# Attention with padded leftover keys, fixed banks and a written order, ahead of two expert stages

## The chip, the core and the metric

The kernel runs on one core of a Trainium2 chip. The core has TensorE (PE; its weight loads are PEld), VectorE (DVE), ScalarE (ACT), GpSimd (POOL), and SyncE (SP), which issues most DMAs. Each runs its own queue in order. The metric is the device time of one execution in microseconds, lower is better.

## The reference

```python
def _attn_ref(q, k, v):                     # each (4, 8, 576, 64)
    # rotate q and k by position (cos and sin tables over the two halves of 64)
    scores = scale * np.matmul(q_rot, k_rot.transpose(0, 1, 3, 2))
    scores = scores - np.max(scores, axis=-1, keepdims=True)
    attn = np.exp(scores)
    attn = attn / (np.sum(attn, axis=-1, keepdims=True) + 1e-09)
    return np.matmul(attn, v)

def _moe_ref(x, w_gate, w_val, w_out):      # x (2304, 512), weights to 1536
    gate = 1.0 / (1.0 + np.exp(-(x @ w_gate)))
    return gate * (x @ w_val) @ w_out

def _moe2_ref(x, w_gate, w1, w2):           # 8 experts, one for each token
    # choose the expert by argmax of x @ w_gate; out = its weight * relu(x @ w1[e]) @ w2[e]
```

The attention's result, with its heads side by side, is the 2304 x 512 input of the gate stage, whose result is the input of the routed experts.

## The kernel before

Every product is made of rounded operands: a value is split into a high part (`hi`, a cast to the rounded type) and a low part (`lo`, the difference), and two or three products are added in PSUM.

The attention works on 16 pairs of heads (`Pair`). Each kind of work on a pair is a piece with a letter:

- `L` loads q, k or v; `K` and `A` rotate k and q (`rope`), `D` copies the rotated k beside itself, `B` and `C` make q's high and low parts, `w` and `G` those of v (tile `vs`).
- `q0` to `q4` transpose the rotated k and q on TensorE, `c` and `b` split the result into `kh` and `kl` and cast it to `qz`.
- `s0` to `s8` are the scores of 128 queries against 576 keys (`s8`: the last 64 queries of both heads), two products for each half of 288 keys. `m` is the row maximum on VectorE, `e` the exponential on ScalarE, which also gives the row sums.
- `t0` to `t10` transpose the probabilities P, `h` casts them to `Th`, `d` takes the difference `Tl`. `t1` and `t6` are those of the last 64 queries, which lie for head 0 on rows 0 to 63 and for head 1 on rows 64 to 127 of one tile (`p` in the rows).
- `v` (head 0) and `o` (head 1) are the output products, ten for each half of 288 queries. The 576 keys are four blocks of 128 rows (tiles `Tha`, `Thb`) and 64 leftover keys of both heads, one above the other in one tile (`Thc`, `Tlc`). So the first two of the ten are products with 64 rows. A half group of five is `v0`, `v1` and so on.
- `z`, `r`, `y`, `Y`, `Z` bring the reciprocal sums through DRAM (`rd`, `rb`) to the layout of the output, `l`, `a`, `F` finish it (`x`), `X` stores it to `xs` in DRAM. `U` is a step of the preparation of the gate stage's first weights.

The order is written by hand as tables of pieces with a lag in pairs (`FIRST`, `STEADY`, `LAST`) and holds for all five engines. PSUM has eight banks: two that rotate for P (`tp`), twice two for scores (`S`), two for q, k and outputs (`O`). The rotation tables (`tab`, four planes) come in three DMAs, and all first loads go through SP's queue.

The gate stage (`moe1`) takes x from `xs` in tiles of 384 tokens (`xr`, split into `xh` and `xl`) and multiplies with weights that are loaded as 64-bit words (`wraw`) and decoded on VectorE. Its first block is three tiles. SP's order and the other engines' order behind the attention are a scheduler's.

Of the kernel before, what the change touches and what calls it, by code (L numbers as in the profile page):

```python
# [11 lines left out]
F32 = mybir.dt.float32  # L12
# [23 lines left out]
FIRST = """  # L36
    s5:1 F:2 A:-1 e4:1 q3:0 m5:1 h4:2 c3:0 s6:1 t5:3 d10:3 b1:0 h9:3 d6:2 m6:1 e5:1 q2:0 h8:3 l3:3 s7:1 m7:1
    e6:1 q4:0 s8:1 m8:1 h7:3 D:-1 h5:2 t2:1 B:-1 c4:0 c2:0 v0:3 t10:3 h10:2 e7:1 w:0 C:-1 d7:2 h6:3 Lq:-2 b4:0
    h2:1 d2:1 v2:3 t3:1 s0:0 o2:3 m0:0 t0:1 h3:1 d8:2 U:2 e8:1 d4:3 K:-2 o3:2 h0:1 d3:1 Y:2 e0:0 X:3 s1:0 m1:0
    Lk:-3 d5:3 Lv:0 z:1 a3:2 t4:3 a2:3 q0:-1 s2:0 d0:1 e1:0 t1:1 a0:2 v3:2 h1:1 l1:2 t6:3 t7:2 d9:2 q1:-1 a1:2  # L40
    r:1 s3:0 t8:3 c0:-1 y:1 G:0 o1:3 Z:2 m2:0 e2:0 d1:1 v1:2 l0:2 o0:3 s4:0 m3:0 t9:3 e3:0 l2:2 c1:-1 b0:-1 m4:0
"""
STEADY = """
    D:-1 A:-1 t4:2 h4:2 s5:1 b1:0 t5:2 q4:0 e4:1 F:3 q3:0 d4:2 c4:0 h5:2 s6:1 c3:0 t7:2 b4:0 m5:1 h7:2 q2:0 v0:2
    d5:2 B:-1 m6:1 t6:2 e5:1 Y:2 h6:2 d7:2 e6:1 K:-2 v1:2 X:3 s7:1 t10:2 d6:2 t9:2 Lq:-2 l0:2 U:1 c2:0 s8:1
    Lk:-3 m7:1 h10:2 a0:2 d10:2 e7:1 h9:2 q0:-1 v2:2 m8:1 t8:2 c0:-1 s0:0 d9:2 v3:2 e8:1 h8:2 l1:2 s1:0 G:1
    b0:-1 m0:0 Z:2 t0:1 d8:2 e0:0 m1:0 o0:2 Lv:-1 h0:1 e1:0 a1:2 w:0 t1:1 s2:0 o2:2 d0:1 t3:1 s3:0 m2:0 h1:1
    h3:1 o1:2 e2:0 C:-1 z:1 d1:1 t2:1 m3:0 l2:2 d3:1 h2:1 e3:0 o3:2 s4:0 a2:2 d2:1 m4:0 r:1 l3:2 q1:-1 y:1 c1:-1
    a3:2
"""  # L50
# [1257 lines left out]
```

## Time and profile before

| what | us |
|---|---|
| median of three runs | 1125.86 (1122.24 to 1130.41) |
| the profiled execution | 1121.85 |
| its span, first to last instruction | 1120.1 |
| TensorE busy in the span | 1085.5 |
| VectorE busy | 739.7 |
| ScalarE busy | 544.1 |
| GpSimd busy | 308.5 |

The times are device time; the profile is of one execution, and its span is measured from its first instruction. An engine's busy time is the time in which at least one of its instructions was being executed. The matmuls are pipelined, so that printed lengths on TensorE overlap.

### The profile page before, as it was taken

The page shows a single profiled execution, that of the slowest core. Times are in us where ns is not written, and L with a number is a line of the kernel's source. Part 1 is how long each engine was busy: PE and PEld are TensorE (multiplying, and loading weights), DVE is VectorE, ACT ScalarE, POOL GpSimd, SP SyncE. Part 2 cuts the span into 40 slices and gives each one's busy share as a digit, 9 for nine tenths or more (in the row PEclk, how much of TensorE's full clock was granted, in tenths as well). Part 3 has the DMA queues.
Part 4 walks back from the last instruction along what each step waited for, and adds up shares of the span by engine and source line. Part 5 has one row for each costly group of instructions (what it writes and reads, how often), then busy time and mean ns, then how long its engine had stood idle before and what let it go on. Part 6 is the DMA issues. An engine that isn't in the chain of part 4 may idle for free. (4 is left out here: it accounts for less than half of the span.)

```text
span 1120.1 us, 18566 instructions
## 1 busy us (share of the span) xinstructions
PE 1085.5 (97%) x6349; PEld 962.2 (86%) x6349; DVE 739.7 (66%) x1581; ACT 544.1 (49%) x1164; POOL 308.5 (28%) x281
## 2 busy tenths in 40 slices
PE   6999999999999999999999999999999999999993
PEld 6889888888889999997889999987778888888882
DVE  5898888888887887876657655555672333846620
ACT  4888888888884222233221222232233444856631
POOL 6967576675211000000100100001215322222200
PEclk8999999999999999999999999999999999999997
DMA  6434233341125344342134332120122615757400
GB/s 176 107 80 112 65 107 104 85 108 54 54 71 163 114 148 126 121 137 61 30 67 74 105 108 81 57 85 20 49 67 59 226 45 183 262 179 288 148 20 19
DMA packets 86101, 116.74 MB, mean 104 GB/s; under 512 B 29727, under 2 KB 71071, under 8 KB 81904
## 3 DMA queue, kind: packets, MB, share of 16 engines
q1 hardware_dynamic: 80864, 104.08, 30.2%
q0 software_dynamic: 5136, 11.40, 3.1%
q8 instruction: 52, 0.85, 0.4%
q14 instruction: 49, 0.40, 0.2%
HBM read 168.33 MB, written 15.70 MB: 164 GB/s over the span
## 5 line engine op out<-in xcount | busy, mean ns | idle before, releaser
L646 PE MATMUL z<-xh,zh 128*128 128x384 f32 x576 | 194.1, 337 | 0.0
L646 PE MATMUL z<-xl,zh 128*128 128x384 f32 x576 | 193.7, 336 | 0.0
L729 POOL DMA_INDIRECT idx<-tokid,pi x18 | 19.6, 1086 | 433.7 <-DVE pi L728 372.5
L646 PE MATMUL z<-xh,zl 128*128 128x384 f32 x576 | 123.8, 336 | 0.3 <-DVE zl L554 0.3
L202 DVE TENSOR_REDUCE nm<-S 128x1 f32<-128x576 f32 x144 | 107.8, 749 | 21.4 <-PE S L199 20.4
L646 PEld LDWEIGHTS z<-xl,zh 128*128 128x128 f32 x576 | 108.2, 188 | 0.9 <-DVE xl L528 0.8
L646 PEld LDWEIGHTS z<-xh,zh 128*128 128x128 f32 x576 | 108.2, 188 | 0.1
L646 PEld LDWEIGHTS z<-xh,zl 128*128 128x128 f32 x576 | 101.9, 188 | 0.9 <-DVE zl L554 0.9
L211 ACT ACTIVATE P<-S,nm 128x576 f32<-128x576 f32 x128 | 95.4, 745 | 7.5 <-DVE nm L202 6.4
L652 ACT ACTIVATE sg<-z 128x384 f32<-128x384 f32 x72 | 35.2, 489 | 117.3 <-PE z L646 106.7
L653 DVE TENSOR_TENSOR g<-z,sg 128x384 f32<-128x384 f32 x72 | 40.0, 556 | 75.1 <-PE z L646 75.1
L670 PE MATMUL xm<-oh,gh 128*128 128x512 f32 x216 | 88.5, 410 | 0.0
L670 PE MATMUL xm<-oh,gl 128*128 128x512 f32 x216 | 84.6, 392 | 0.0
L670 PE MATMUL xm<-ol,gh 128*128 128x512 f32 x216 | 84.5, 391 | 0.0
L199 PE MATMUL S<-kh,qz 128*128 128x288 f32 x320 | 78.3, 326 | 4.2 <-ACT P L211 3.2
L527 ACT CAST gh<-g 128x512 fp32r<-128x512 f32 x54 | 33.3, 621 | 91.8 <-PE xm L670 87.2
L249 PE MATMUL tp<-ident,P 128*128 128x128 f32 x512 | 74.8, 274 | 0.3 <-DVE Tla L270 0.3
L1124 PE MATMUL y<-w2h,hh 128*128 128x512 f32 x176 | 72.5, 412 | 1.7 <-ACTq L1144 0.9
L1009 DVE TENSOR_TENSOR xl<-tp,xh 128x512 fp32r<-128x512 f32 x21 | 14.5, 691 | 85.2 <-ACT xh L1008 48.9
L1124 PE MATMUL y<-w2l,hh 128*128 128x512 f32 x176 | 69.4, 394 | 0.0
L1124 PE MATMUL y<-w2h,hl 128*128 128x512 f32 x176 | 68.9, 392 | 0.0
L199 PE MATMUL S<-kl,qz 128*128 128x288 f32 x320 | 68.8, 296 | 0.0
(241 smaller groups left out, 2648.4 us busy)
## 6 DMA issues: line engine op xcount, KB each, us to landing
raw<-in_moe_w_dram SPq DMA_DIRECT2D x100, 1024.0 KB
wraw<-in_moe_w_gate_dram SPq DMA_DIRECT2D x23, 512.0 KB
wraw<-in_moe_w_val_dram SPq DMA_DIRECT2D x23, 512.0 KB
wraw<-in_moe_w_out_dram SPq DMA_DIRECT2D x12, 512.0 KB
rb<-rd SPq DMA_DIRECT2D x32, 144.0 KB
xs<-x SPq DMA_DIRECT2D x16, 288.0 KB
xr<-xs SPq DMA_DIRECT2D x24, 192.0 KB
ldk<-in_k_dram SPq DMA_DIRECT2D x16, 256.0 KB
```

The lines of the kernel that those rows point to most:

```text
L199: nc.tensor.matmul(ps[:, c, 0:288], st, t[:, 288 * c:288 * c + 288], start=(n == 0), stop=(n == len(ops) - 1))
L202: nc.vector.tensor_reduce(out=self.nm[:, u:u + 1], in_=self.S[u][:, :, 0:288], axis=AX.XY, op=ALU.max, negate=True)
L211: nc.scalar.activation(out=p.rearrange("p (a b) -> p a b", a=2), in_=self.S[u][:, :, 0:288], func=AF.Exp, bias=self.nm[:, u:u + 1], accum_ ...
L249: nc.tensor.transpose(ps[:, 128 * i:128 * i + 128], P[i][:, h, c:c + 128], ident)
L527: nc.scalar.copy(out=hi, in_=src)
L646: nc.tensor.matmul(p[:, 0:TN], a[:, 128 * c:128 * c + 128], b[:, c], start=(n == 0), stop=(n == 11))
L652: nc.scalar.activation(out=sg, in_=z[0], func=AF.Sigmoid)
L653: nc.vector.tensor_tensor(out=g[i][:, f], in0=z[1], in1=sg, op=ALU.mult)
L670: nc.tensor.matmul(p, a[:, c], b[f], start=(f == 0 and m == 0), stop=(f == NF - 1 and m == 2))
L729: nc.gpsimd.indirect_dma_start(out=idx, out_offset=bass.IndirectOffsetOnAxis(ap=pi, axis=0), in_=tokid[:, blk:blk + 1], in_offset=None)
L1009: self.nc.vector.tensor_tensor(out=lo, in0=src, in1=hi, op=ALU.subtract)
L1124: nc.tensor.matmul(py, a[:, c], b[:, c], start=(c == 0 and m == 0), stop=(c == 7 and m == 2))
```

## The change

- The 64 leftover keys of a head are padded to a block of 128 rows. v is loaded to a tile of two times five blocks with zeros in the other head's half (`ldv`), so that a leftover product takes all 128 rows of `Thc` with `vs` zero in the other head's rows. The leftover queries of both heads are transposed together in full 128-row blocks (`t1`, `t6`), and the transpose of the sums (`r`) becomes the third block of `t6`, its copy (`y`) a part of `h6`. For this `kh` and `kl` keep the shared leftover keys twice (one more copy in `c4`, one more difference in `b4`).
- The rotating PSUM tiles become four single banks and two double ones, and each piece has its bank in the order (`/n`).
- The order is one written list of 1675 pieces for all pairs.
- Only the two planes of k's rotation table are loaded; ScalarE makes q's from them and copies them for the second head. The small first loads of k and q go out on ScalarE's queue. Pair 0's q is rotated in two parts (`J`, `I`, `N` are the second head's).
- v's high part for all pairs but the first is cast on GpSimd (`W`), and so are both parts of the gate stage's first weights.

```diff
-FIRST = """
-    s5:1 F:2 A:-1 e4:1 q3:0 m5:1 h4:2 c3:0 s6:1 t5:3 d10:3 b1:0 h9:3 d6:2 m6:1 e5:1 q2:0 h8:3 l3:3 s7:1 m7:1
...
+ORDER = """
+    K.0 J.0 A.0 D.0 Lk.2 q1.0/0 q0.0/1 c1.0 Lq.2 B.0 b1.0 K.1 c0.0 C.0 W.0 b0.0 q2.0/2 I.0 q4.0/3 G.0 c2.0 c4.0 N.0 Lv.2
...
+    t10.15/2 h7.15 d6.15 v0.15/1 h10.15 d7.15 X.14 t9.15/3 d10.15 t8.15/0 h9.15 v1.15 h8.15 d9.15 v2.15/2 l0.15 d8.15 v3.15
+    Z.15 a0.15 o0.15/3 l1.15 o1.15 a1.15 o2.15/0 l2.15 o3.15 a2.15 l3.15 a3.15 F.15 X.15
...
-    ps_t = ctx.enter_context(tc.tile_pool(name="a_pt", bufs=2, space=PSUM))
-    ps_s = ctx.enter_context(tc.tile_pool(name="a_ps", bufs=2, space=PSUM))
-    ps_o = ctx.enter_context(tc.tile_pool(name="a_po", bufs=2, space=PSUM))
+    ps = ctx.enter_context(tc.tile_pool(name="a_ps", bufs=1, space=PSUM))
+    BANK = [ps.tile([128, 512], F32, name=f"bank{i}") for i in range(4)]
+    BANKS = [ps.tile([128, 2, 512], F32, name=f"banks{i}") for i in range(2)]
...
+        def L_(self, nm, parts=(0, 1), g=nc.sync):
+            src = {"q": q, "k": k, "v": v}[nm]
+            s = src[self.b, 2 * self.hp:2 * self.hp + 2]
+            if nm == "v":
+                t = ldv[self.i % 2]
+                nc.sync.dma_start(out=t[:, :, 0:4].rearrange("p h u d -> p h (u d)"),
                                   in_=s[:, 0:512].rearrange("h (p u) d -> p h (u d)", u=4))
+                for h in range(2):
+                    nc.sync.dma_start(out=t[64 * h:64 * h + 64, h, 4], in_=s[h, 512:576])
+                return
...
+        def W_(self, n):
+            self.vs = sb_o.tile([128, 10, 2, 64], F32R, tag="vs", name="vs", bufs=3)
+            src = ldv[self.i % 2].rearrange("p h u d -> p (h u) d")
+            if self.i == 0:
+                nc.scalar.copy(out=self.vs[:, :, 0], in_=src)
+            else:
+                nc.gpsimd.tensor_copy(out=self.vs[:, :, 0], in_=src)
...
         def t_(self, g):
-            ps = self.tp[g] = ps_t.tile([128, 512], F32, tag="tp", name="tp")
+            ps = self.tp[g] = BANK[self.slot]
+            blocks = lambda n: ps[:, 128 * n:128 * n + 128]
...
-            elif g == 1 or g == 6:
-                h = 0 if g == 1 else 1
-                p = slice(64 * h, 64 * h + 64)
+            elif g == 1:
+
                 for j in range(4):
-                    c = 64 + 64 * h + 128 * j
-                    nc.tensor.transpose(ps[:, 64 * j:64 * j + 64], P8[p, c:c + 128], ident[p, p])
-                c = (576, 0)[h]
-                m = (64, 128)[h]
-                nc.tensor.transpose(ps[0:m, 256:320], P8[p, c:c + m], ident[p, p])
+                    nc.tensor.transpose(blocks(j), P8[:, 128 * j:128 * j + 128], ident)
+            elif g == 6:
+
+                nc.tensor.transpose(blocks(0), P8[:, 512:640], ident)
+                nc.tensor.transpose(blocks(1), P8[:, 448:576], ident)
+                nc.tensor.transpose(ps[0:9, 256:384], self.r, ident)
...
         def v_(self, n, h=0):
...
-                if j == 4:
-                    p = slice(64 * h, 64 * h + 64)
-                    st, mv = self.vs[p, 8], T[2][p, cs]
-                else:
-                    st, mv = self.vs[:, 4 * h + j], T[h][:, j, cs]
+                mv = T[2][:, cs] if j == 4 else T[h][:, j, cs]
+                st = self.vs[:, 5 * h + j]
...
-        nc.sync.dma_start(out=tab[:, 2:4, 4:9], in_=rope_tab[:, 2:4])
-        p0.load("k")
-        nc.sync.dma_start(out=tab[:, 0:2, 4:9], in_=rope_tab[:, 0:2])
-        p0.load("q")
-        p1.load("k")
-        nc.sync.dma_start(out=tab[:, :, 0:4], in_=rope_tab[:, :, 0:4])
+        nc.sync.dma_start(out=tab[:, 2:4, 4:9], in_=rope_tab)
+        p0.L_("k", (1,), nc.scalar)
+        p0.L_("k", (0,))
+        p0.L_("q", (1,), nc.scalar)
+        p0.L_("q", (0,))
+
+        nc.scalar.mul(out=tab[:, 0:2, 4:9], in_=tab[:, 2:4, 4:9], mul=SCALE)
+        nc.scalar.copy(out=tab[:, 2:4, 0:4], in_=tab[:, 2:4, 4:8])
+        nc.scalar.copy(out=tab[:, 0:2, 0:4], in_=tab[:, 0:2, 4:8])
...
+        for piece in ORDER.split():
+            x, i, slot = (piece.replace("/", ".") + ".-1").split(".")[:3]
+            i = int(i)
+            pairs[i].slot = int(slot)
+            getattr(pairs[i], x[0] + "_")(x[1:] if x[0] == "L" else int(x[1:] or 0))
...
-        self.steps += [lambda: nc.scalar.copy(out=w.hi, in_=val),
-                       lambda: nc.vector.tensor_tensor(out=w.lo, in0=val, in1=w.hi, op=ALU.subtract)]
+        self.steps += [lambda: nc.gpsimd.tensor_copy(out=w.hi, in_=val),
+                       lambda: nc.gpsimd.tensor_tensor(out=w.lo, in0=val, in1=w.hi, op=ALU.subtract)]
```

In the steady part TensorE's queue of the kernel before has, in one place, a half of the outputs of head 1, the leftover transposes of one head and the next scores:

```order
L309 MATMUL O<-Thc,vs 128x288
L309 MATMUL O<-Tlc,vs 128x288
L309 MATMUL O<-Thb,vs 128x288
L309 MATMUL O<-Tlb,vs 128x288
L309 MATMUL O<-Thb,vs 128x288
L241 MATMUL tp<-ident,p_112 128x64 x4
L244 MATMUL tp<-ident,p_112 64x64
L199 MATMUL S<-kh,qz_111 128x288 x2
L199 MATMUL S<-kl,qz_111 128x288 x2
```

A like place of the changed kernel on TensorE, where the outputs lie in bank 102 and the leftover transposes in bank 100:

```order
L420 MATMUL bank_102<-Thc,vs 128x288
L420 MATMUL bank_102<-Tlc,vs 128x288
L420 MATMUL bank_102<-Thb,vs 128x288
L420 MATMUL bank_102<-Tlb,vs 128x288
L420 MATMUL bank_102<-Thb,vs 128x288
L274 MATMUL bank_99<-ident,rk 128x128
L274 MATMUL bank_99<-ident,rq 128x128
L363 MATMUL bank_100<-ident,p_112 128x128
L364 MATMUL bank_100<-ident,p_112 128x128
L365 MATMUL bank_100<-ident,r 9x128
```

The five small transposes became two full ones and that of the sums; the number of output products is the same.

At the end of the attention SP's queue of the kernel before reads x for the gate stage (`xr`) between the attention's own transfers:

```order
L292 DMA rb<-rd 64x576 x2
L634 DMA xr<-xs 128x384 x8
L373 DMA xs<-x 128x576
L634 DMA xr<-xs 128x384 x3
L542 DMA wraw<-in_moe_w_gate_dram 128x4x256
L542 DMA wraw<-in_moe_w_val_dram 128x4x256
L285 DMA rd<-rt 4x2x128
L286 DMA rd<-rt 2x1x64
```

and SP's queue of the changed kernel there:

```order
L400 DMA rd<-rt 4x2x128
L401 DMA rd<-rt 2x1x64
L447 DMA xs<-x 128x576
L407 DMA rb<-rd 64x576 x2
L703 DMA xr<-xs 128x384 x4
L611 DMA wraw<-in_moe_w_gate_dram 128x4x256
L611 DMA wraw<-in_moe_w_val_dram 128x4x256
L447 DMA xs<-x 128x576
L611 DMA wraw<-in_moe_w_gate_dram 128x4x256
L703 DMA xr<-xs 128x384
L838 DMA wglr<-in_moe_w_gate_dram 128x4x8
L703 DMA xr<-xs 128x384 x7
```

The last sums' write and read (`rd`, `rb`) moved ahead of all xr loads, and eight of the twelve stand behind the last store of x.

## Rows read from the trace of the kernel before

**Rows 1.** Busy time by stage: us, each engine (instructions), clock, DMA share, GB/s.

```profile
0.00:20.00 20.00, 12.98 (x82) 11.82 (x83) 9.45 (x25) 6.55 (x12) 9.87 (x17) 0.89 0.67 199
...
100.00:200.00 100.00, 99.35 (x729) 88.22 (x727) 86.87 (x160) 86.47 (x217) 68.96 (x61) 1.00 0.35 95
```

**Rows 2.** Waits from 60 to 330 us: us in total, times, longest.

```profile
DVE nm L202 <- PE S L199: 15.2, 26, 0.7
...
PEld tp L249 <- DVE Tla L270: 0.8, 2, 0.6
```

**Rows 3.** Timeline of TensorE in one pair: start, length, what, count.

```profile
192.44 0.29 PE L309 MATMUL O<-Thb,vs 128*128 128x288 f32 x1
192.66 0.46 PE L241 MATMUL tp<-ident,p 64*128 64x64 f32 x4
...
193.47 0.42 PE L199 MATMUL S<-kl,qz 128*128 128x288 f32 x2
193.83 0.40 PE L309 MATMUL O<-Thc,vs 64*128 64x288 f32 x1
...
194.66 0.29 PE L309 MATMUL O<-Thb,vs 128*128 128x288 f32 x1
194.79 0.60 PE L249 MATMUL tp<-ident,P 128*128 128x128 f32 x4
...
195.50 0.43 PE L199 MATMUL S<-kl,qz 128*128 128x288 f32 x2
...
196.42 0.60 PE L249 MATMUL tp<-ident,P 128*128 128x128 f32 x4
...
198.06 0.27 PE L274 MATMUL tp<-ident,r 128*9 128x128 f32 x1
198.16 0.60 PE L146 MATMUL O<-ident,rk 128*128 128x128 f32 x4
```

**Rows 4.** Line 149 (one a pair) from 60 to 310 us: first and last start.

```profile
L149 PE MATMUL O<-ident,rk x13: 272/273/273, 60.7 to 299.6; 128*128 128x128 f32 x13
```

**Rows 5.** Timeline of VectorE in the steady stretch.

```profile
102.33 0.68 DVE L270 TENSOR_TENSOR Tla<-tp,Tha 128x512 fp32r<-128x512 f32 x1
102.93 0.75 DVE L202 TENSOR_REDUCE nm<-S 128x1 f32<-128x576 f32 x1
```

**Rows 6.** Timeline of the head; in brackets idle time before and what ended it.

```profile
1.75 0.72 SPq L105 DMA_DIRECT2D ldk<-in_k_dram  x1
...
4.67 0.69 DVE L122 TENSOR_TENSOR rk<-ldk,tab 128x512 f32<-128x512 f32 x1 [3.09 <-DMA ldk<-in_k_dram]
...
7.34 0.23 DVE L122 TENSOR_TENSOR rk<-ldk,tab 128x64 f32<-128x64 f32 x1 [1.31 <-DMA ldk<-in_k_dram]
...
9.02 0.69 DVE L122 TENSOR_TENSOR qs<-ldq,tab 128x512 f32<-128x512 f32 x1 [0.45 <-DMA ldq<-in_q_dram]
...
15.11 0.71 PE L146 MATMUL O<-ident,rq 128*128 128x128 f32 x4 [2.51 <-DVE kl L181]
...
19.05 0.85 PE L199 MATMUL S<-kh,qz 128*128 128x288 f32 x2 [1.01 <-ACT qz L174]
```

**Rows 7.** Change-over to the gate stage: timelines, and line 646 by stage.

```profile
324.86 11.69 SPq L634 DMA_DIRECT2D xr<-xs  x8
...
330.52 0.51 ACT L527 CAST xh<-xr 128x384 fp32r<-128x384 f32 x1
...
344.58 0.67 SPq L285 DMA_DIRECT2D rd<-rt  x1
...
345.88 0.29 PE L309 MATMUL O<-Tlb,vs 128*128 128x288 f32 x1
...
347.02 1.15 SPq L292 DMA_DIRECT2D rb<-rd  x2
...
356.50 0.55 DVE L653 TENSOR_TENSOR g<-z,sg 128x384 f32<-128x384 f32 x1
...
330.00:346.00 16.00, 4.74 (x19) 3.22 (x20) 1.00 0.57 171
```

More of the change, by code (lines that the diff above doesn't have):

```diff
@@ L61 @@
+"""
+FIRST_HEAD = (slice(0, 4), slice(8, 9))
+SCALE = 1.0 / np.sqrt(D)
 WARM = {"": 40, "q0": 20}
@@ L121, in rope @@
-            for (iv, ov, wv), (c, s) in zip(parts, tabs):
+            for n in blocks:
+                two = self.i == 0 and n == slice(0, 8)
+                sh = (lambda x: x[:, n].rearrange("p (h u) d -> p h u d", h=2)) if two else (lambda x: x[:, n].unsqueeze(1))
+                at = slice(4, 8) if n.stop in (4, 8) and self.i == 0 else n
+                c, s = (tab[:, ti + x, at].unsqueeze(1) for x in range(2))
+                if two:
+                    c, s = (x.to_broadcast([128, 2, 4, 64]) for x in (c, s))
+                iv, ov, wv = sh(t), sh(o), sh(w)
@@ new lines, in J_, with high, low, B_ @@
+        def J_(self, n):
+            self.q_tiles()
+            self.rope(nc.gpsimd, "q", self.qs, (slice(4, 8),))
+        def high(self, g, blocks):
+            o = self.rq4[:, :, 0].bitcast(F32R)
+            for n in blocks:
+                g(out=o[:, n], in_=self.qs[:, n])
+        def low(self, g, blocks):
+            for n in blocks:
+                g.tensor_tensor(out=self.rq4[:, n, 1], in0=self.qs[:, n], in1=self.rq4[:, n, 0], op=ALU.subtract)
+        def B_(self, n):
+            self.high(nc.gpsimd.tensor_copy if self.i else nc.scalar.copy, FIRST_HEAD if not self.i else (slice(0, 9),))
@@ new lines, in C_, with I_, N_ @@
+        def C_(self, n):
+            self.low(self.g(), FIRST_HEAD if not self.i else (slice(0, 9),))
+        def I_(self, n):
+            self.high(nc.scalar.copy, (slice(4, 8),))
+        def N_(self, n):
+            self.low(nc.vector, (slice(4, 8),))
+        def W_(self, n):
[3 more added lines that the diff above has]
+                nc.scalar.copy(out=self.vs[:, :, 0], in_=src)
+            else:
+                nc.gpsimd.tensor_copy(out=self.vs[:, :, 0], in_=src)
@@ L169, in c_ @@
             if g < 2 or g == 4:
-                src, hi, _ = self.k_parts(g)
-                nc.scalar.copy(out=hi, in_=src)
+                for src, hi, _ in self.k_parts(g):
+                    nc.scalar.copy(out=hi, in_=src)
             if g in (2, 3):
@@ L205, in e_ @@
             if u == 8:
-                p = self.P8[:, 64:640]
+                p = self.P8[:, 0:576]
             else:
@@ L375, in attention @@
     pairs = [Pair(i) for i in range(npairs)]
-    nxt = {}
-    def run(slot, order):
-        for x, lag in order:
-            while nxt.get(x, 0) <= min(slot - lag, npairs - 1):
-                p = pairs[nxt.get(x, 0)]
-                nxt[x] = p.i + 1
-                getattr(p, x[0] + "_")(x[1:] if x[0] == "L" else int(x[1:] or 0))
-                if p.i == 0:
-                    warm(WARM.get(x, 0))
-    head, steady, last = ([(a.split(":")[0], int(a.split(":")[1])) for a in l.split()] for l in (FIRST, STEADY, LAST))
-    ET = mybir.EngineType
     def warm(n):
         for _ in range(n):
-            nc.tensor.transpose(ps_w[:, 0:128], ident, ident)
-    ps_w = ps_t.tile([128, 512], F32, tag="tp", name="warm")
+            nc.tensor.transpose(BANK[3][:, 0:128], ident, ident)
+    ET = mybir.EngineType
     with tc.manual_schedule(engines={ET.PE, ET.Activation, ET.DVE, ET.Pool, ET.SP}):
```

306 lines of the change are left out of this document (165 added, 141 removed).

## The prediction

> **What bounds the kernel now.** I read the table by stage first. In the attention's steady stretch [rows 1] TensorE is marked busy 99.35 of 100 us at full clock (1.00, the 2.4 GHz level), VectorE and ScalarE 87 and 86, GpSimd 69. One pair of heads takes (299.6 - 60.7) / 12 = 19.9 us [rows 4]. A busy mark does not say that TensorE does useful work all that time, so I went on to the waits: between 60 and 330 us TensorE waited 0.8 us in all for a bank of transposed P, while VectorE waited 15.2 us for scores [rows 2]. The others wait for TensorE. Then I read TensorE's own timeline by the distance from one start to the next, since the printed lengths overlap [rows 3]. The reader is to see there that products of one kind follow each other every 0.13 us, transposes every 0.11 us, and that the distances jump to 0.2 us and more around everything that uses only 64 rows. After 357 us come the two expert stages, where TensorE stays full; the change does not touch them, and what the attention gains or loses arrives at the end one for one, as long as their first loads come in time.
>
> **The change part by part.**
>
> Padding of the leftover keys. The stretch from 193.47 to 194.79 holds two score products and the five products of a half-group that begins with the two 64-row ones: 1.32 us. The stretch from 195.50 to 196.42 holds two score products and five full ones: 0.92 us [rows 3]. So a half-group with 64-row products costs 0.40 us more, though it has the same number of products and columns. Each pair has four such halves (two heads, two column halves): 1.6 us. The leftover transposes: from the last product before them to the second score product behind them it is 193.47 - 192.44 = 1.03 us, and 195.50 - 194.66 = 0.84 us around four full transposes [rows 3], so five 64-row ones cost 0.19 us more than four full ones. Of the two groups the first becomes four full ones (0.19), the second two and the sums' transpose, which stood elsewhere at 198.16 - 198.06 = 0.10: 0.19 + 0.10 + 0.10 = 0.39. Together 2.18 us a pair; I take 2.1, since two decimals are at the edge of what these rows give. The sum over 16 pairs: **-33.6 us**. A padded product adds nothing: the full ones beside it, with 128 rows, are the cheap ones.
>
> The Trainium skill, "TensorEngine Tiling (Array Packing)", Key Properties, speaks against this edit: tiles of a smaller array "operate independently" and can load and multiply in parallel, so 64-row products would be the cheap ones and padding would give that up. The trace disagrees: the 64-row products of one head stand one behind the other, and the stretch that holds them is the longer one. By that rule the term would be 0 instead of -33.6 us.
>
> What is late next. With 2.1 us less, TensorE needs 17.8 us a pair at the waits of now. VectorE is busy 86.87 of 100 us, 17.3 us a pair [rows 1], and the change gives it one more small subtraction (the copied leftover keys). Its printed lengths overlap as well: a difference printed as 0.68 us is followed by the next start after 0.60 [rows 5]; with some 30 instructions a pair its real need lies between 15 and 17.3 us. So it would work 85 to 98% of the new period in one queue in which each instruction waits for TensorE or ScalarE. Some of the gain will go into new waits of TensorE: at least 0, at most what comes if VectorE, with some 17.5 us of marked work a pair, cannot be filled above 92% (it stands at 87 now; this is an estimate from that row): 17.5 / 0.92 = 19.0 us a pair, 1.2 us more than 17.8, times 14 steady pairs = 17 us. I take 0.4 us a pair, nearer to the lower end because the waits of now are near zero on TensorE's side: **+6 us** (0 to +17). ScalarE loses the cast of v, which goes to GpSimd, and gains a small copy: it stays behind VectorE. GpSimd has 31 us of 100 free [rows 1] and takes one cast more and a slightly larger subtraction a pair: nothing, unless it were late with the low part of v, for which its queue has one pair of lead. The fixed banks: the same eight banks, four of them now shared by q, P and the outputs; nothing while TensorE's bank waits stay at 0.8 us in 270 [rows 2]. That is bounded by the fourth case below.
>
> The head. The first score product starts at 19.05 us [rows 6]. On its way lie: k's last 64 rows, issued third at 1.75 us, for which VectorE stands still until 7.34 us (1.31 us); q, which is behind a second table of 327 KB and lands at 9.02; a rotation, split and two casts of all 576 rows; and TensorE's 2.51 us until VectorE frees the bank for q's first transposes [rows 6]. The change issues the small pieces first on ScalarE's queue, makes the second table on ScalarE from the first, drops the third, and takes only q's first head and the leftovers before the first score. 327 KB at 199 GB/s [rows 1] are 1.6 us; VectorE's wait is 1.3; half of the rotation, the split and the casts of q and the wait for the bank are worth about 2 more. New on that path: the scaling, which hides before k lands, and the cast of v for pair 0 on ScalarE, which now waits for v's load ahead of three casts. I take **-5 us**, between -2.5 (VectorE's wait and the halved work of one engine) and -6.5 (all of it).
>
> Of the two queues the Trainium skill, "DMA: Bandwidth & Descriptors", Issuing engines are not separate DMA queues, says that issuing from several engines saves only the sequencer's time, since all transfers share the same 16 engines. By it the small pieces would gain their 0.72 us of issue [rows 6] rather than VectorE's 1.3 us, and the term would be -4.4 us.
>
> The change-over. Now 19 products of the gate stage already run between the attention's last ones [rows 7], the eight loads of xr they need are issued from 324.86 on, used from 330.52, and the stage's first block of three tiles ends at 356.50, 10.6 us after the attention's last product at 345.88. In the new program no such product stands before the attention's last, and SP has only four xr loads ready, behind the read of the last sums (rb); the other eight come after the last x store, which waits for the attention's end. The 19 products are no loss in themselves: their 3.3 us then lie outside the attention. What is lost is waiting. The read rb comes 347.02 - 344.58 = 2.4 us after the sums' write and takes 1.15 us to issue [rows 7]; between that write and the end the new order has three groups of transposes and eight half-products, some 6.6 us by the distances of [rows 3]. So the four loads go out 3 us before the end, and the first can be used 330.52 - 324.86 = 5.7 us after its issue at the latest, 2.7 us past the end. Eight more follow beside weight loads. I take **+4 us**, from 0 (all hidden) to +9 (5.7 for the second batch and 3 for its rows one after the other).
>
> Sum, against the profiled execution's 1121.85 us: -33.6 + 6 - 5 + 4 = -28.6, so 1093.3. The three timed runs begin at 1122.24 and have their median at 1125.86, 4 us above it; I add half of that and say **1095 us**.
>
> **The rivals.**
>
> First, VectorE becomes the bound: 19.0 us a pair. For it speaks its share of 87%; against it that it still idles 13 us of 100, and mostly for TensorE's scores, which would come sooner. The time: 1121.85 - 33.6 + 17 - 5 + 4 = 1104.
>
> Second, the change-over gives back more: xr and the first weights come so late that the gate stage's first block stalls for 9 us or more. For it speaks the one queue of SP on which the last x store holds what is behind it. Time: 1121.85 - 33.6 + 6 - 5 + 9 = 1098, and with the first rival 1109.
>
> Third, the page's rule: 64-row products already hide in their neighbours, and padding saves nothing. Against it stand the two stretches of [rows 3]. Time: 1121.85 + 0 + 0 - 5 + 4 = 1121.
>
> Fourth, on the other side: TensorE stands at its banks. A piece has one bank by number now and the order is fixed, so a difference on VectorE that comes late stops TensorE and all that is behind. Each pair takes a bank 20 times (5 for q and k, 11 for P, 4 for outputs). The edits together are worth 33.6 + 5 - 4 = 34.6 us, 2.2 us a pair; from 0.11 us of wait at each taking on the kernel gets slower. At 0.15 us it is 3.0 x 16 = 48 us more: 1121.85 - 34.6 + 48 = 1135. For it speaks VectorE's load; against it that today's pairs of P banks cost 0.8 us in 270 [rows 2], and there are four now.
>
> **How the numbers follow.** The forecast (steady period 17.9 to 18.6 us) has 0.60, VectorE as the bound 0.20, the change-over 0.06, both of these together 0.06, the page's rule 0.03, the banks 0.05. The range: the lower end is the sum with all bounds at their best, -33.6 + 0 - 6.5 + 0, which gives 1082; the upper takes +17, -2.5 and +9: -10.1, so 1112. That leaves out the last two cases and a part of the fifth. A measurement of this kernel tells about 1% from no change: 1114.6 to 1137. The first four cases lie below that, the rule inside, the banks at its upper edge or past it: 0.89 faster, 0.07 the same, 0.04 slower.
>
> **What the profile of the changed kernel would show.** Padding: no stretch of seven products longer than about 0.95 us by starts, and a period from one leftover transposition of q and k to the same one a pair later of 17.9 to 18.6 us on average; 19.0 would be the first rival. VectorE's busy share in the steady stretch should go up to 92 to 97%. The head: the first score product at 13 to 16 us. The change-over: from the attention's last product to the last result of the first gate block 15 to 19 us instead of 10.6. Later stages: same lengths as before. I am wrong if the two stretches do not shorten (the rule), if TensorE's waits for banks reach microseconds per pair (the banks), or if the expert stages take longer than now.

## The result, and the profile after

| | before | after |
|---|---|---|
| median | 1124.05 us (4 runs, 1121.87 to 1130.41) | 1109.19 us (4 runs, 1104.51 to 1110.90) |
| profiled execution, its span | 1121.85, 1120.1 | 1104.51, 1102.7 |

The ratio is 0.9844, 95% interval 0.9812 to 0.9877: 1.6% faster (the two medians divided give 0.987). The forecast of 1095 us was too good by 14 us; the range held. The ratios in this document leave out slow executions, of which there was one: 2691 us, among the eight of e2. In the profiled executions the gain is 17.3 us of the 26.9 forecast (28.6 by its own terms).

**The steady stretch.** Busy time by stage of the kernel after, then its waits from 60 to 330 us (the attention's last product is at 316), columns as in [rows 1, 2].

```profile
20.00:60.00 40.00, 35.89 (x273) 33.57 (x272) 33.93 (x62) 35.56 (x90) 39.03 (x38) 0.98 0.39 111
60.00:100.00 40.00, 39.58 (x315) 38.41 (x313) 38.46 (x72) 36.27 (x96) 39.02 (x36) 1.00 0.39 103
100.00:200.00 100.00, 98.03 (x769) 93.90 (x768) 94.29 (x181) 90.68 (x238) 82.96 (x75) 1.00 0.37 105
```
```profile
ACT P L332 <- DVE nm L323: 9.3, 21, 1.0
...
DVE nm L323 <- PE banks L320: 3.2, 7, 0.8
...
PEld bank L370 <- DVE Tlb L395: 2.1, 5, 0.6
...
PEld bank L370 <- DVE Tla L395: 1.6, 4, 0.6
```

TensorE is still marked busy 98 of 100 us, but VectorE has gone from 87 to 94 and ScalarE from 86 to 91. The direction of waiting has turned: VectorE's wait for scores fell from 15.2 us [rows 2] to 3.2, and ScalarE now waits 9.3 us for VectorE's maxima (2.7 before). TensorE waits in small pieces for VectorE: the listed waits of its weight loads between 60 and 290 us add up to 9.5 us, 0.8 us a pair, where before they were 7.1 us, 0.6 a pair. None of them is longer than 0.7 us.

TensorE's timeline answers [rows 3]: two score products, then five of a half-group that begins with the leftover ones.

```profile
80.90 0.42 PE L320 MATMUL banks<-kl,qz 128*128 128x288 f32 x2
81.16 0.29 PE L420 MATMUL bank<-Thc,vs 128*128 128x288 f32 x1
81.30 0.30 PE L420 MATMUL bank<-Tlc,vs 128*128 128x288 f32 x1
81.43 0.29 PE L420 MATMUL bank<-Tha,vs 128*128 128x288 f32 x1
81.56 0.29 PE L420 MATMUL bank<-Tla,vs 128*128 128x288 f32 x1
81.70 0.30 PE L420 MATMUL bank<-Tha,vs 128*128 128x288 f32 x1
81.83 0.60 PE L271 MATMUL bank<-ident,rk 128*128 128x128 f32 x4
```

All starts are 0.13 us apart, and the seven products take 81.83 - 80.90 = 0.93 us where they took 1.32.

**The head.** VectorE (DVE) and GpSimd (POOL) on the way to the first score, from the timeline.

```profile
6.07 0.69 DVE L198 TENSOR_TENSOR rk<-ldk,tab 128x512 f32<-128x512 f32 x1 [4.57 <-DMA ldk<-in_k_dram]
...
7.65 1.09 POOL L198 TENSOR_TENSOR qs<-ldq,tab 128x256 f32<-128x256 f32 x1 [5.56 <-DMA ldq<-in_q_dram]
8.07 0.75 DVE L198 TENSOR_TENSOR rk<-ldk,tab 128x64 f32<-128x64 f32 x1
...
9.96 2.23 DVE L201 TENSOR_TENSOR rw<-ldq,tab 128x128 f32<-128x128 f32 x2
10.58 1.46 POOL L198 TENSOR_TENSOR rk<-ldk,tab 128x576 f32<-128x576 f32 x1
12.01 1.78 POOL L201 TENSOR_TENSOR rw<-ldk,tab 128x288 f32<-128x288 f32 x2
12.23 0.91 DVE L202 TENSOR_TENSOR qs<-qs,rw 128x256 f32<-128x256 f32 x1
```

The first score product stands at 19.13 us (before 19.05). k's main load lands 1.4 us later than before (6.07 for 4.67 in [rows 6]), and the same 128x64 multiplication that took 0.23 us before takes 0.75 here, beside GpSimd.

**The change-over.** SyncE's queue, ScalarE's split of x, TensorE, and the first gate block's last result; then the same stretch by stage.

```profile
312.78 2.00 SPq L703 DMA_DIRECT2D xr<-xs  x4
...
320.17 0.34 SPq L447 DMA_DIRECT2D xs<-x  x1
...
322.16 6.52 SPq L703 DMA_DIRECT2D xr<-xs  x7
```
```profile
325.67 2.04 ACT L596 CAST xh<-xr 128x384 fp32r<-128x384 f32 x4 [6.47 <-DMA xr<-xs]
...
326.24 0.44 PE L715 MATMUL z<-xh,zh 128*128 128x384 f32 x1 [2.41 <-ACT xh L596]
...
338.59 0.56 DVE L722 TENSOR_TENSOR g<-z,sg 128x384 f32<-128x384 f32 x1 [0.34 <-PE z L715]
```
```profile
320.00:326.00 6.00, 3.22 (x17) 2.90 (x17) 0.56 (x1) 0.33 (x1) 0.14 (x1) 1.00 0.99 321
326.00:332.00 6.00, 5.61 (x19) 4.70 (x20) 4.55 (x11) 5.12 (x10) 0.00 (x0) 0.72 0.47 141
```

Four loads of `xr` bring one tile of 384 tokens. SyncE's last store of x goes out at 320.17, and all eight loads for the second and third tile stand behind it. ScalarE waits 6.5 us for them, TensorE 2.4 us, and TensorE's clock then averages 0.72 for 6 us, between its levels of 2.4 and 1.2 GHz.

**Where the gain came and went.** Five marks split the time: the first score product, the first of pair 2 and of pair 15 (the 81st and 601st of 640), the last attention product, and the last product of the first gate block (the 72nd z). The period is the 13 pairs from pair 2 to pair 15, divided by 13.

| us | first score | pair 2 | pair 15 | period | last attention product | first gate block done |
|---|---|---|---|---|---|---|
| before | 19.05 | 49.78 | 308.36 | 19.89 | 345.88 | 355.72 |
| after | 19.13 | 49.70 | 287.71 | 18.31 | 316.02 | 338.14 |

By these marks nothing is gained up to pair 2 (0.1 us). The 13 steady pairs give 20.6. From pair 15's first score to the end of the first gate block the kernel after needs 50.4 us where the kernel before needed 47.4: 3.1 are given back. Sum 17.6; behind that mark both need the same (764.4 and 764.6 us).

The marks of the two orders do not enclose the same work, though. Counted in the traces, TensorE has made 40 output products when pair 2 begins, in the kernel before 15; from there to pair 15 it makes 505 in place of 520, and behind it 95 in place of 105. At 0.13 us each, and with four transposes of k fewer at 0.11, the kernel after is about 2.8 us of work ahead at pair 2 (an estimate from these distances). So the sum is better split where the work is the same: the first score comes 0.1 us later; from it to the last attention product it is 296.9 us, where before it was 326.8 with 3.3 us of gate products among them (the 19 of [rows 7] at 0.17 us), so the 16 pairs give 26.6 us; and the change-over takes back 9.0, as worked out below.

### The profile page after: what moved, and what is told of

Read it like the earlier page. It is cut to its first block, busy times and chain, and to the rows that moved or that the text cites. A ratio compares the mean times of both kernels' runs of the same rounds, so it can differ in the third digit from the quotient of the medians.

```text
span 1102.7 us, 18492 instructions
## 1 busy us (share of the span) xinstructions
PE 1059.9 (96%) x6285; PEld 958.3 (87%) x6285; DVE 739.2 (67%) x1599; ACT 537.8 (49%) x1167; POOL 325.5 (30%) x305
## 5 line engine op out<-in xcount | busy, mean ns | idle before, releaser
L323 DVE TENSOR_REDUCE nm<-banks 128x1 f32<-128x576 f32 x144 | 107.6, 747 | 10.8 <-PE banks L320 8.3
L332 ACT ACTIVATE P<-banks,nm 128x576 f32<-128x576 f32 x128 | 96.5, 755 | 12.3 <-DVE nm L323 11.3
L320 PE MATMUL banks<-kh,qz 128*128 128x288 f32 x320 | 78.5, 326 | 2.1 <-ACT P L332 2.1
L370 PE MATMUL bank<-ident,P 128*128 128x128 f32 x512 | 74.5, 275 | 3.4 <-DVE Tlb L395 1.0
L320 PE MATMUL banks<-kl,qz 128*128 128x288 f32 x320 | 69.0, 297 | 0.1
```

Of the source, the lines that this page charges most:

```text
L320: nc.tensor.matmul(ps[:, c, 0:288], st, mv[:, 288 * c:288 * c + 288], start=(n == 0), stop=(n == len(ops) - 1))
L323: nc.vector.tensor_reduce(out=self.nm[:, u:u + 1], in_=self.S[u][:, :, 0:288], axis=AX.XY, op=ALU.max, negate=True)
L332: nc.scalar.activation(out=p.rearrange("p (a b) -> p a b", a=2), in_=self.S[u][:, :, 0:288], func=AF.Exp, bias=self.nm[:, u:u + 1], accum_ ...
L370: nc.tensor.transpose(blocks(i), P[i][:, h, c:c + 128], ident)
```

## The experiments

By the record two chips ran these, one e1 to e4 and the other e5 to e12. The kernel before takes 1142.33 us on the one and 1138.21 (a single run) or 1141.19 us on the other. The kernel after, traced again there as e12, has the attention's marks of its first trace within 2 us, and longer expert stages. So whole times are compared by the ratio to the kernel before on the same chip, and pieces by their marks. e4 to e8 were run once each. Two traces of one kernel, after and e12, differ by 0.85 us at pair 2 and by 1.2 us from pair 15's first score to the end of the first gate block (50.4 and 51.7), so a microsecond between single traces tells little.

| kernel | first score | pair 2 | pair 15 | period | last attention product | first gate block done |
|---|---|---|---|---|---|---|
| e1 unpadded | 19.09 | 52.35 | 303.57 | 19.32 | 334.69 | 356.40 |
| e2 before, padded | 17.81 | 47.93 | 292.62 | 18.82 | 328.47 | 349.27 |
| e3 last transfers on GpSimd | 19.38 | 49.93 | 287.90 | 18.31 | 316.20 | 333.80 |
| e4 one load queue | 18.46 | 50.74 | 288.29 | 18.27 | 316.58 | 338.83 |
| e5 more TensorE | 19.09 | 50.63 | 298.28 | 19.05 | 329.24 | 350.52 |
| e6 more VectorE | 19.31 | 51.95 | 313.27 | 20.10 | 343.43 | 365.83 |
| e7 more ScalarE | 19.22 | 49.67 | 302.36 | 19.44 | 331.85 | 354.61 |
| e8 GpSimd later in the head | 16.27 | 49.32 | 287.62 | 18.33 | 315.93 | 338.18 |
| e9 no addition | 19.29 | 50.99 | 287.02 | 18.16 | 315.21 | 337.49 |
| e10 e3, pools swapped | 19.46 | 51.53 | 289.07 | 18.27 | 317.37 | 335.13 |
| e11 e9 and e10 together | 18.08 | 49.79 | 285.80 | 18.15 | 313.99 | 331.75 |
| e12 after again | 18.76 | 50.55 | 288.33 | 18.29 | 316.63 | 339.98 |

### e1: the padding undone

```diff
-                mv = T[2][:, cs] if j == 4 else T[h][:, j, cs]
-                st = self.vs[:, 5 * h + j]
+                p = slice(64 * h, 64 * h + 64) if j == 4 else slice(0, 128)
+                mv = T[2][p, cs] if j == 4 else T[h][:, j, cs]
+                st = self.vs[p, 5 * h + j]
```

> One edit to the kernel after: the leftover products of the output (two in each of the four groups of a pair) use 64 rows again; all else stays. Theory A (padding is the gain and TensorE sets the period): the products around them are spread as before, 0.40 us in each of four groups, so the period of a pair goes from 18.3 to about 19.9 us and the whole time up by 20 to 25 us, to 1125 to 1132. Theory B (VectorE sets the period of the kernel after): TensorE's own slack of about 1.2 us a pair swallows most of it, the period rises by 0.3 to 0.6 us and the time by 4 to 9 us, to 1109 to 1115. Theory C (products of 64 rows run side by side, as the Trainium skill has it on the page TensorEngine Tiling): no change or a gain, 1100 to 1106.

Measured: 1142.01 us beside 1142.33, ratio 1.0005 (0.9988 to 1.0023): the whole gain is gone. TensorE's timeline shows why.

```profile
198.18 0.43 PE L320 MATMUL banks<-kl,qz 128*128 128x288 f32 x2
198.54 0.40 PE L421 MATMUL bank<-Thc,vs 64*128 64x288 f32 x1
198.77 0.29 PE L421 MATMUL bank<-Tlc,vs 64*128 64x288 f32 x1
198.99 0.40 PE L421 MATMUL bank<-Thb,vs 128*128 128x288 f32 x1
199.23 0.30 PE L421 MATMUL bank<-Tlb,vs 128*128 128x288 f32 x1
199.37 0.29 PE L421 MATMUL bank<-Thb,vs 128*128 128x288 f32 x1
199.50 0.29 PE L421 MATMUL bank<-Tlb,vs 128*128 128x288 f32 x1
```

The two 64-row products, and the first full one behind them, stand 0.22 to 0.24 us from their neighbours, the others 0.13. From the score products to the sixth product it is 1.32 us again. Over all such half-groups between 60 and 290 us, the time from the start ahead of the five products to the start behind them has a median of 1.184 us (48 of them), with padding 0.796 (50): 0.39 each, as the prediction's 0.40. Four a pair make 1.56 us, but the period rises by only 1.01 (18.31 to 19.32), and the end of the first gate block comes 18.3 us later. Theory C is out; the price is theory A's, and a third of it is swallowed, so that the answer lies between A and B.

### e2: the padding alone, on the kernel before

```diff
-            self.vs = sb_o.tile([128, 9, 2, 64], F32R, tag="vs", name="vs", bufs=3)
+            self.vs = sb_o.tile([128, 10, 2, 64], F32R, tag="vs", name="vs", bufs=3)
...
-                    p = slice(64 * h, 64 * h + 64)
-                    st, mv = self.vs[p, 8], T[2][p, cs]
+                    st, mv = self.vs[:, 8 + h], T[2][:, cs]
```

The raw v lies in two fixed buffers whose unused halves are zeroed once.

> One part of the change alone on the kernel before: the leftover rows of v are stored as two blocks of 128 rows with zeros, and the leftover products use all 128 rows; the order, the PSUM pools, the leftover transposes and the head stay as before (at the very end one piece of the last pair but one stands five pieces later). Theory A (TensorE is the bound, 0.40 us in each of four groups): the period goes from 19.9 to about 18.3 us and the time from 1121.9 down by 20 to 25 us, to 1097 to 1102, so that all the rest of the change gave nothing or cost some microseconds. Theory B (the old order keeps VectorE and TensorE waiting for each other, so the padding can be used only with the new order): the period stays above 19.2 us and the time above 1110.

Measured: 1135.33 us (median of seven), ratio 0.9952 (0.9931 to 0.9972). The period fell from 19.89 to 18.82, by 1.07 us, the same step as in e1, and lies between what the two theories expected. But from pair 15's first score to the end of the first gate block this kernel needs 56.7 us, where the kernel before needs 47.4: 9.3 are lost at the change-over. Neither theory has this. The kernel's instruction order shows a difference: 19 products of the gate stage stand ahead of the attention's last product before, and none here, though the attention's own order is the same but for one piece. With that piece left in its place the order has none either, and the kernel before with only that piece moved still has 19 (neither was run). The scheduler places the gate stage's pieces itself, and the new buffers of v were enough to move them. So in the old order too this part of the change-over's price comes with the padding's buffers; how much of the 9.3 us it is was not separated.

### e3: the last transfers on GpSimd

```diff
+            e = nc.gpsimd if self.i == 15 else nc.sync
-                nc.sync.dma_start(out=self.rbt[64 * h:64 * h + 64], in_=d[h:h + 1].to_broadcast([64, S]))
+                e.dma_start(out=self.rbt[64 * h:64 * h + 64], in_=d[h:h + 1].to_broadcast([64, S]))
```

The same in `Y_` for pair 15, and in `X_` for pairs 14 and 15.

> In the kernel after, the transfers that belong to the end of the last two pairs (the sums of pair 15 to and from memory, the stores of x of pairs 14 and 15) are issued by GpSimd in place of SyncE, so that the loads of the gate stage don't queue behind them. Theory A (the change-over costs 9 us because SyncE stands in the wait for the last store until 320.2 us, and the loads of the second and third block behind it start only at 321): these loads start at 316 to 318 us, TensorE's wait of 2.4 us at 326 us goes, its clock stays at 1.00 through 326 to 332, and 3 to 6 us come back, 1099 to 1102 beside 1104.5. Theory B (the loads wait for their places in SBUF, which free only as the first block has been split, and not for the queue): the loads start no more than 1 us earlier and the time stays within 1 us of the kernel after.

Measured: 1121.19 us, ratio 0.9833 (0.9799 to 0.9867); the kernel after stands at 0.9844 on its own chip and at 0.9871 in e12, on the other, and the intervals overlap, so the whole times do not settle it. The first gate block ends at 333.80 us, 4.3 earlier than in the kernel after. SyncE's queue, then the two stages by busy time:

```profile
315.30 2.35 SPq L706 DMA_DIRECT2D xr<-xs  x4
317.70 0.42 SPq L841 DMA_DIRECT2D wglr<-in_moe_w_gate_dram  x1
322.47 1.84 SPq L706 DMA_DIRECT2D xr<-xs  x4
```
```profile
320.00:326.00 6.00, 4.60 (x18) 3.40 (x17) 2.88 (x6) 4.29 (x7) 1.98 (x2) 0.85 0.81 258
326.00:332.00 6.00, 5.48 (x25) 4.64 (x24) 6.00 (x15) 1.93 (x5) 0.00 (x0) 0.86 0.14 48
```

Theory A holds in its main step: the second tile's loads went out at 315.3 in place of 321 to 322, and 4.3 us came back, between the 3 and 6 expected. It overstated the rest: TensorE still waits 1.25 us at 321.9, and its clock averages 0.85 over these 12 us, no better than the 1.00 and 0.72 of the kernel after.

### e4 and e8: the head

In e4 SyncE issues all first loads (`p0.L_("k")`, `p0.L_("q")` in place of the four calls). In e8 GpSimd's part of pair 0's rotation waits for VectorE's:

```diff
-    K.0 J.0 A.0 D.0
+    K.0 A.0 J.0 D.0
...
             self.q_tiles()
+            nc.gpsimd.tensor_copy(out=self.rq4[:, 8, 1, 0:1], in_=self.qs[:, 8, 0:1])
             self.rope(nc.gpsimd, "q", self.qs, (slice(4, 8),))
```

> In the kernel after, the first loads of pair 0 are all issued by SyncE again (table, k, k's leftover rows, q, q's leftover rows), none by ScalarE. Theory A (the small loads of 64 floats a row on ScalarE's queue held up the table and the main load of k, which landed 1.4 us later than in the kernel before): the table lands before 4.0 us, the first VectorE operation starts at about 4.7 us, and the first S product comes at 17.5 to 18.3 us in place of 19.13. Theory B (the slower operations of VectorE beside GpSimd are what ate the gain): the loads' landing moves but the first S product stays at 18.6 to 19.6 us.

> In the kernel after, GpSimd's share of the rotation of pair 0's q and its rotation of pair 1's k begin only when VectorE has rotated its share of q (a copy of one column on GpSimd waits for it). Theory A (VectorE's small operations are slow because GpSimd works beside them): the two multiplications of 128x128 that took 2.23 us take about 0.3 to 0.7, the 128x64 ones 0.23 in place of 0.75 to 0.81, and the first S product comes 3 to 5 us earlier, at 14 to 16 us, which is where the prediction put it. Theory B (they are slow by themselves, or by the transfers that land): the durations stay, and the first S product is at 18.5 to 19.5 us.

Measured: e4 1124.74 us, e8 1122.80. VectorE's first operation on k in e4:

```profile
5.24 0.69 DVE L198 TENSOR_TENSOR rk<-ldk,tab 128x512 f32<-128x512 f32 x1 [3.75 <-DMA ldk<-in_k_dram]
```

In e4 the table lands at 4.4 us (5.2 in the kernel after), VectorE starts at 5.24 (6.07), and the first score comes at 18.46, 0.7 us earlier: between its two theories. But ten traces here have the head of the kernel after (after, e1, e3, e5 to e7, e9 to e12); in them VectorE starts at 5.59 to 6.50 us and the first score comes at 18.08 to 19.46. So e4's start of VectorE lies outside that spread, by 0.35 us, and its first score inside. That the small loads on ScalarE's queue hold up the others is suggested by one trace, and a gain at the first score is not shown. Pair 2 begins at 50.74 (50.55 in e12), and the first gate block ends at 338.8. In e8 VectorE's timeline is another:

```profile
8.24 0.22 DVE L198 TENSOR_TENSOR rk<-ldk,tab 128x64 f32<-128x64 f32 x1
...
9.17 0.49 DVE L201 TENSOR_TENSOR rw<-ldq,tab 128x128 f32<-128x128 f32 x2
...
10.04 0.21 DVE L198 TENSOR_TENSOR qs<-ldq,tab 128x64 f32<-128x64 f32 x1
```

0.22 in place of 0.75 us, 0.49 in place of 2.23, 0.21 in place of 0.81: the operations are slow only beside GpSimd, as theory A of e8 says, and the first score comes at 16.27 us, 2.9 earlier. Yet pair 2 begins at 49.32 (0.4 earlier, 1.2 beside e12) and the first gate block ends at 338.18, as in the kernel after. The trace shows where the gain went: GpSimd, then ScalarE and TensorE of e8.

```profile
17.31 1.40 POOL L202 TENSOR_TENSOR rk<-rk,rw 128x576 f32<-128x576 f32 x1
...
18.73 0.67 ACT L212 COPY rk<-rk 128x576 f32<-128x576 f32 x1 [1.59 <-POOL rk L202]
...
19.46 1.09 PE L272 MATMUL bank<-ident,rk 128*128 128x128 f32 x8 [1.89 <-ACT rk L212]
```

GpSimd's rotation of pair 1's k, which e8 itself put later, ends at 18.7 us (15.3 in the kernel after), and TensorE waits 1.9 us behind it. After that its clock averages 0.61 and 0.54 from 20 to 28 us, where the kernel after has 0.82 and 1.00. So this early first score was swallowed by what e8 put off; whether one without that price would reach the end is open.

### e5, e6, e7: which engine the steady stretch waits for

e5 adds 12 transposes a pair on TensorE, e6 and e7 four copies on VectorE and on ScalarE; results nobody reads. The line of e6 (e7 has the same on ScalarE, e5 three `nc.tensor.transpose` behind each output group):

```diff
+            l = slice(64 - 64 * h, 128 - 64 * h)
+            nc.vector.tensor_copy(out=self.L[n][l], in_=tab.rearrange("p a b c -> p (a b c)")[l, 0:288])
```

> In the kernel after, 12 more transposes a pair on TensorE (three behind each of the four output groups, into columns of its bank that nobody reads): about 12 times 0.109 = 1.3 us of TensorE a pair. The period of a pair was 18.31 us. Theory A (TensorE sets the period, the others have room): 19.3 to 19.6. Theory B (VectorE, 94% busy, sets it): 18.4 to 18.7. Theory C (no engine alone: each waits in turn for another, all three over 90%): 18.7 to 19.2.

> In the kernel after, four more copies a pair on VectorE (64 rows by 288 columns, SBUF to SBUF, into the half of the L tiles that nobody reads, one behind each of the four additions of the output): 0.6 to 1.6 us of VectorE a pair, to be read from the trace. Theory A (TensorE sets the period, VectorE is 94% busy and has 1.1 us of room): the period of 18.31 us rises by less than a third of the added time. Theory B (VectorE sets it): by nearly all of it. Theory C (mixed): by about half.

> In the kernel after, four more copies a pair on ScalarE (64 rows by 288 columns into the half of the L tiles that nobody reads, one behind each of the four copies of the output): by the row of those copies 0.40 us each, 1.6 us a pair. ScalarE was 91% busy, 1.6 us of room in a period of 18.31 us. Theories A and B (TensorE or VectorE sets the period): it rises by less than 0.5 us. Theory C (mixed): by 0.6 to 1.0 us. All of it, 1.6 us, if ScalarE is what the order waits for.

The added operations by line, e6 and then e7, 60 to 290 us (count, busy us, mean ns; in e6 also shortest, median and longest):

```profile
L438 DVE COPY L<-tab 64x288 f32<-64x288 f32 x44 | 21.3, 484 | 1.4
...
L438 DVE COPY L<-tab x44: 301/308/1589, 68.4 to 277.9; 64x288 f32<-64x288 f32 x44
```
```profile
L430 ACT COPY L<-tab 64x288 f32<-64x288 f32 x48 | 20.7, 432 | 1.2
```

| added to a pair | us added | period | rise | share that comes through |
|---|---|---|---|---|
| TensorE, 12 x 0.109 | 1.31 | 19.05 | 0.74 | 56% |
| VectorE, 4 x 0.484 | 1.94 | 20.10 | 1.79 | 92% |
| ScalarE, 4 x 0.432 | 1.73 | 19.44 | 1.13 | 65% |

The whole times are 1137.50, 1155.66 and 1142.01 us beside 1138.21 of the kernel before. Theory A is out: VectorE's marked time comes through nearly whole. Theory B fails too, by the other two: TensorE's and ScalarE's added work raises the period by more than B allows, so no engine has its full slack to spare. Theory C, that each waits in turn for another, stands best, but not by its figures: e5 falls into its range, e7's 1.13 us lies above its 0.6 to 1.0, and e6's 92% above its half. And e6 added more than work. Of its 44 copies 30 took 0.30 to 0.38 us, the other 14 took 0.43 to 1.59 us, and each of the 14 began while an operation of GpSimd ran (as did 10 of the short ones). At the median of 0.308 us the four copies are 1.23 us, less than the 1.79 by which the period rose. So VectorE's queue is what the pair waits for most, but how near to the bound its own work stood, e6 does not tell.

### e9: work taken from VectorE

```diff
-            nc.vector.tensor_scalar_add(r, self.sums, 1e-9)
-            nc.vector.reciprocal(out=r, in_=r)
+            nc.vector.reciprocal(out=r, in_=self.sums)
```

> In the kernel after, one VectorE operation a pair is left out: the addition of 1e-9 to the sums of the softmax, which are at least 1, ahead of their reciprocal (0.27 us by its row in the trace of the kernel after). Theory B, as the runs that added work have it (VectorE's time comes through at 92%): the period of 18.31 us falls by about 0.25 us, to 18.05, and the end of the first gate block comes 3 to 4.5 us earlier. Theory A (VectorE has room): the period stays within 0.05 us.

Measured: 1123.91 us, ratio 0.9849 (0.9826 to 0.9872) beside 0.9871 of e12; the period fell by 0.15 of the 0.27 us that the row gives:

```profile
L337 DVE TENSOR_SCALAR r<-sums 128x9 f32<-128x9 f32 x11 | 2.9, 268 | 1.4 <-ACT P L332 1.2
```

That is less than theory B's 0.25 us and more than theory A's 0.05; beside e12's period it is 0.13. The intervals of e9 and e12 overlap, so in the whole time nothing is shown. VectorE added comes through at 92%, VectorE removed at 56%: that the others bind as soon as VectorE has less to do would explain it, and was not tested.

### e10, e11, e12: the pools swapped, all together, and the base

e10 is e3 with the pools `a_in` and `a_k` made in the order of before; e11 is e10 and e9 together; e12 is the kernel after.

> The kernel after with the last pairs' transfers on GpSimd (as in e3) and the two SBUF pools of attention's inputs in the order of the kernel before, so that the gate stage's tiles lie on the buffers of the raw and rotated q and k, which come free early, and no longer on the split k, which TensorE reads up to the last S product. Theory A (part of what the change-over still costs is that wait, 4.2 us on the loads of x in e3): the first loads end at about 301 us in place of 305.8, and the end of the first gate block comes 1 to 4 us earlier than in e3 (333.8 us). Theory B (those loads are early enough, and the order of ScalarE, which splits x only after attention's last casts, decides): no more than 0.5 us.

> The three edits together on the kernel after: the last pairs' transfers on GpSimd, the two input pools swapped back, the addition of 1e-9 left out. If their gains add (4.3 us for the transfers, 3 to 4.5 us for the addition, 0 to 4 for the pools), the first gate block ends at 326 to 331 us in place of 338.1, and the whole is 7 to 12 us below the kernel after: a ratio of 0.973 to 0.979 to the kernel before. If VectorE's room is eaten by another engine, 0.980 or more.

> The kernel after, unchanged, on the chip and against the runs of the kernel before that the other runs of this group share, as their base. By the first measurement its ratio is 0.9844; expected 0.981 to 0.988, with the first gate block's end at 338 us.

Measured: e10 1122.66 us, 0.9835 (0.9807 to 0.9863); e11 1119.19, 0.9800 (0.9777 to 0.9822); e12 1126.97, 0.9871 (0.9847 to 0.9895). In e10 SyncE's first four loads are issued in one stretch (the first row); in e3 (the second) they took until 305.75, with 4.2 us of waiting for the last score products:

```profile
301.05 1.98 SPq L706 DMA_DIRECT2D xr<-xs  x4
```
```profile
299.88 5.87 SPq L706 DMA_DIRECT2D xr<-xs  x4
```

But from pair 15's first score to the end of the first gate block e10 needs 46.1 us and e3 45.9: theory B, these loads were early enough already. e11 beats both kernels, the kernel after by 7.8 us of the medians, with intervals that don't meet. At the end of the first gate block it is 8.2 us ahead of e12: 5.7 in the change-over (46.0 us from pair 15's first score, 51.7 in e12; beside the 50.4 of the kernel after's first trace it would be 4.5), 1.8 in the steady pairs, the rest ahead of pair 2, where one kernel's two traces differ as much. That misses the expectation for gains that add (0.973 to 0.979, the block's end at 326 to 331 us) and falls on its other case, 0.980 or more. e12 fell into its expected ratio, with the block's end 2 us later than expected.

## Why the prediction was right, and where it was too good

**Padding: right in mechanism, and what reached the end was smaller.** 0.39 us a half-group (e1) for 0.40. By the trace the 64-row products do not run side by side. The rule of the Trainium skill, "TensorEngine Tiling (Array Packing)", Key Properties, speaks of different tiles working in parallel; the two products of a half-group take the same 64 rows (`p` is one slice in the edit of e1), so it does not apply to them, and the 0 that the prediction drew from it did not come. Why the distances grow at these products no run shows. On TensorE the four half-groups are 1.56 us a pair; at the end of a pair 1.0 of it arrives, in either order (e1, e2).

**The new waits on VectorE's side: right.** The forecast period was 17.9 to 18.6 us and VectorE's share 92 to 97%; measured 18.31 and 94%. Padding and waits together were to give 1.7 us a pair and gave 1.58. By e1 1.0 of that is the padding of the output products. The rest, 0.6 by e1 and 0.5 by e2, belongs to the leftover transposes, the banks, the order and the cast of v on GpSimd, which were not tried apart. From the first score to the last attention product the 16 pairs gave 26.6 us where the forecast's terms make 27.6. The first rival (VectorE alone the bound at 19.0 us) named the right engine, as e6 shows, but its 19.0 was too high: VectorE is filled to 94.3%, 17.3 us of marked work a pair, where the bound took 17.5 us at 92%. The rival of the banks is out: it needed 2.2 us of new waits a pair, and the weight loads' waits for VectorE are 0.8. Its comparison was too low, though. The prediction went by 0.8 us of bank waits in 270, which are those of P's banks alone; the bank of q's and k's transposes had a row of its own in the kernel before, from 60 to 330 us:

```profile
PEld O L146 <- DVE kl L181: 3.6, 13, 0.3
```

Nor did VectorE idle mostly for scores: these 15.2 us were half of its some 30 us of listed waits there.

**The head: the step that failed.** The prediction took -5 us from a first score at 13 to 16 us. It came at 19.13. The step gave half of q's rotation to GpSimd as a saving, and did not ask what VectorE and GpSimd do to each other: several rows of VectorE beside GpSimd are 3 to 5 times as long as the same ones in e8. This agrees with the Trainium skill, "SBUF — State Buffer", SBUF: two separate sides, which calls the port that the two share an exclusive lock under which "the other fully blocks". That the small loads on ScalarE's queue cost time where the step counted a saving is suggested by e4 alone. The step also counted what the first score gains as a gain at the end; in e8 a gain of 2.9 us was swallowed before pair 2, but by a wait that e8 itself made. So what an early first score is worth stays open. The head is 5.1 of the missing 11 us.

**The change-over: mechanism right, mis-sized, and at its bound.** The forecast was 15 to 19 us from the last attention product to the last result of the first gate block. It is 338.59 - 316.02 = 22.6. By the last product itself it is 22.1, where before had 9.8 with 19 products (3.3 us) already done [rows 7]: 9.0 us, the bound of the term, for +4: another 5.0 of the missing 11. The sign of 15 to 19 us was missed. The queue behind the last store is the second rival's mechanism, and e3 gives back 4.3 of the 9. The other half of the 9 us is open: e10 rules out the wait for the k tiles, and e2's order shows that the 19 early products vanish with the padding's buffers alone. Why the scheduler moved them was not settled.

By pieces: head forecast -5, measured +0.1; 16 pairs -27.6 and -26.6; change-over +4 and +9.0. That the time still fell into the range was in part luck: the head came out beyond its own bound of -2.5 us, and the 17 us of room left for new waits, which the pairs hardly used, covered it.

## What to carry to other kernels

Where small tiles stand among full ones, measure their price by the distance of starts: padding the 64-row products to 128 took four times 0.39 us off a pair, and undoing it (e1) takes the whole gain away. But a saving on the engine that looks full arrives only as far as its partners can follow, and adding a known piece of work to each engine in turn tells more about which one binds than their busy shares do, if the added piece is not itself held up, as VectorE's copies were beside GpSimd. An earlier start is a gain only if what comes behind is ready for it. Marks of two orders are compared only after counting the work between them. And a queue that ends one stage with a store holds up the loads of the next.

## What the runs showed that I had not expected

VectorE's operations from SBUF to SBUF can get several times as long while GpSimd works, and the profile shows that as busy time and not as a wait: in the head 128x128 twice took 2.23 us beside it and 0.49 alone, and e6's copies up to 1.59 us for 0.30.

TensorE's granted clock falls in the head after it has been idle, and not by the same amount in runs of one head: in the stretches from 16 to 20 and from 20 to 24 us it averages 0.75 and 0.82 in the kernel after (in the 4 us before, TensorE was busy for 1.74), 0.66 and 0.50 in e12, the same kernel (1.35), and 0.55 and 0.60 in e11 (1.22). In e8, with its earlier first score, it is 1.00 from 16 to 20 us, then 0.61 and 0.54 from 20 to 28.
